# The first two blocks of a convolution and SiLU-MLP kernel: convolution on TensorE, w_out loads in a new order, weight sums one by one

## The chip, the cores and the metric

The kernel runs on one core of a Trainium2 chip. A core has five engines that each take their own instructions in order: TensorE (PE in the profile; its weight loads are PEld), VectorE (DVE), ScalarE (ACT), GpSimd (POOL) and SyncE (SP), which here only issues DMAs. An engine waits at an instruction until the semaphores that it names have been raised by other engines or by DMAs that landed. The metric is the device time of one execution in microseconds (us), lower is better; of several runs the median is taken.

## The reference

Two steps follow each other. `x` is 8 x 4096 x 192 float32. A causal depthwise convolution of 7 taps runs along the 4096 positions; the taps are a softmax over 7 weights for each of 8 heads of 24 channels. Its output is a matrix of 32768 x 192, which goes through an MLP of 2048 hidden units with SiLU:

```python
w = np.exp(w); w = w / (np.sum(w, axis=-1, keepdims=True) + 1e-09)      # 8 heads x 7 taps
out = np.einsum('hk,bskhg->bshg', w, x_unf)                             # 7 shifted copies of x
h = x @ w_in                                                            # 32768x192 @ 192x2048
g = h * (1.0 / (1.0 + np.exp(-h)))
return (g @ w_out).astype(np.float32)                                   # 32768x2048 @ 2048x192
```

The weights arrive as float64 and are used in the kernel after a rounding to float32 that it does itself on the two 32-bit halves.

## The kernel before, in words

**Blocks.** The 32768 rows are worked on in 32 blocks of 1024 rows. Of the 192 channels, the first 128 lie on 128 partitions with 1024 rows on the free axis (`k = 0`: tiles `nat0`, `xt0`, `xs0`). The last 64 are folded into 128 partitions by 512 rows (`k = 1`: `nat1`, `xt1`, `xs1`), partitions 0 to 63 for the first 512 rows and 64 to 127 for the second. A block's input is loaded into `nat`, turned by VectorE into `xt` (`turn_in`), convolved (`conv`: one multiply on ScalarE and six multiply-adds on VectorE, in place in `nat`), and split for the float32r matmuls (`split`) into three parts: `h`, a scaled high part, made by ScalarE; `l`, the rest, made by VectorE; and `d`, a correction, made by VectorE.

**Matmuls of a block.** `w_in` gives 16 tiles of 128 hidden units, counted by `j` (0 to 3) and `c` (0 to 3). For each tile, PE adds `A` (channels 0 to 127, parts h and l), `C` (channels 128 to 191, parts h and l), ScalarE rescales the sum in PSUM (`X`), PE adds the corrections `B` and `E`, and ScalarE applies SiLU into `g` (`S`). From block 1 on, A and B too are done in halves of 64 rows, and after C and after E VectorE copies one column of the PSUM bank into `dot` (`T`, `U`); the next matmul that writes that bank waits for this copy. The output product with `w_out` then needs sums of tiles of `g` (`s` tokens) and sums of tiles of `wd` (the rounded `w_out`, made once by `combine_out`), and matmuls `Q`, which for block b stand in the list of block b + 1.

**Order.** From block 1 on, the order of all work is a list of tokens written by hand (`PLAN`), run once for each block by `step`; a token with a minus sign belongs to the block before, one with a plus to the block after. Each engine takes its instructions in the order in which the Python code emits them (`pin`). Block 0 has its own order, lines 671 to 734, since there the weights are still being rounded.

**Block 0.** Its channels 0 to 127 are convolved on PE with seven diagonal matrices of the taps (`diag`), in two PSUM banks (`banks[0]`, `banks[1]`); `split_pe` reads them there. Its channels 128 to 191 are convolved by `conv` on ScalarE and VectorE. Between these stand the rounding units, `Unit`: units 0 to 7 make `w_b` (even units) and `w_a` (odd units) of j = 0 to 3 from `w_in`, units 8 to 11 make a quarter of `wd` each from `w_out`. `work(u)` does one in three pieces: first `begin(u + 1)` (the exponent of the *next* unit, with two operations on POOL and a sign on ScalarE), mantissa and sticky bit; second `rounded`, three VectorE operations, and where so written the issue of a later load; third `split` into three parts and, for `w_b`, two DMAs (`spread`) that copy parts to the other partitions. The raw words of `w_out` come in four loads, `load_out(0)` to `load_out(3)`, of two DMAs each. They reuse buffers: 0 and 3 lie in the same slots of `g`, 1 where the raw words of `w_in`, j = 2, were (`fin[0:6]`), 2 where those of j = 3 were (`fin[6:12]`).

The up products of block 0 are woven with units (`woven`): during j, the four tiles of j (`tile_steps`) and the pieces of units 2j + 3 and 2j + 4. Tiles 0 to 2 have their A done ahead. After the 16 tiles come the last unit, the input of block 1, and the output product of block 0 by 96 plain float32 matmuls (`down_plain`), three copies and transposes into `fin`, and 12 stores. Then `combine_out(0, 1)` puts all 23 sums and two negations of `wd` on VectorE, and the list of tokens starts with block 1.

Of the kernel before, what the change touches and what calls it, by code (L numbers as in the profile page):

```python
# [18 lines left out]
def kernel(  # L19
# [340 lines left out]

    def combine_out(part, parts):
        work = [*COMBINE_OUT, *((0, s, s, s) for s in NEGATE_OUT)]
        n = (len(work) + parts - 1) // parts
        for sign, to, u, v in work[n * part : n * part + n]:
            to, u, v = (wd[:, :, s, :] for s in (to, u, v))
            if sign:
                vec.tensor_tensor(to, u, v, op=ALU.add if sign > 0 else ALU.subtract)
            else:
                vec.tensor_scalar(to, u, scalar1=-1.0, scalar2=None, op0=ALU.mult)

# [224 lines left out]
    units += [Unit(q, ("o", q), None) for q in range(NJ)]  # L595

    def begin(u):
        if u < len(units):
            units[u].exponent()

    def work(u):

        now = units[u]
        begin(u + 1)
        now.mantissa()
        now.sticky()
        yield
        now.rounded()
        if now.key == ("o", 0):
            load_out(3, sync)  # L610
        yield
        if now.part is not None:
            now.split()
            now.spread()
        yield
# [9 lines left out]

    diag = flat(g_all[:, 0, 7])[:, 0 : K * P].rearrange("p (i c) -> p i c", c=P)

# [4 lines left out]
    def of_work(u):  # L632
        stream = work(u)
        for _ in range(3):
            yield lambda: next(stream, None)
# [35 lines left out]

    for i in range(K):
        act.activation(diag[:, i, :], one_hot, AF.Copy, scale=taps[:, 0, i : i + 1])
    turn_in(0, 0)
    for n in range(2):
        for i in range(K):
            mm(banks[n], diag[:, i, :], xts[0][:, n * TB + i : n * TB + i + TB], i == 0)
    homes.append(homes.pop(0))
    homes.append(homes.pop(0))
    begin(0)  # L680
    first_ = work(0)
    next(first_)
# [86 lines left out]
```

## Time and profile before

| | |
|---|---|
| median of 3 runs | 2268.2 us (2267.3 to 2268.77) |
| the profiled execution | 2267.96 us |
| its span, first to last instruction | 2266.2 us |
| PE busy | 2229.3 us, 98% |
| DVE busy | 1831.4 us, 81% |
| ACT busy | 1302.0 us, 57% |
| POOL busy | 59.5 us, 3% |
| mean granted TensorE clock | 0.991 |

The span is cut off by the first and the last instruction; 1.8 us of the profiled execution's time lie outside it. PE is busy nearly throughout, but its busy time holds slow matmuls too: where the granted clock is 0.50, a matmul takes twice as long. In a row of the timeline stand the start and the length in us, the engine, the line, the operation, out<-in, the count, and in brackets the idle time of the engine just before with what ended it. L142 is the helper through which all operations but the matmuls go, so the rows are told apart by their tiles and shapes.

### The profile page before, as it was taken

Reading aid. Unit: us, or ns where it says so; the run is one execution under the profiler, and the core shown is the slowest. Engines: PE = TensorE matmul, PEld = TensorE weight load, DVE = VectorE, ACT = ScalarE, POOL = GpSimd, SP = SyncE. Lnnn points to the kernel's source line nnn. Section 1 sums busy time; section 2 is a strip of 40 time slices with the busy share of each in tenths; the row PEclk is TensorE's granted clock in tenths of the full one; section 3 lists DMA queues with packets and bytes.
Section 4 is the critical chain, followed back from the end, with each engine's and each line's share of the span. In section 5 each row is a group of like instructions: output and inputs, shape, how many; then the busy total and the mean of one; then the engine's idle time right before and its main releaser. Section 6 shows DMA issues by size and latency. Waiting matters only on the chain.

```text
span 2266.2 us, 47061 instructions
## 1 busy us (share of the span) xinstructions
PE 2229.3 (98%) x19276; PEld 1671.2 (74%) x19276; DVE 1831.4 (81%) x3029; ACT 1302.0 (57%) x2671; POOL 59.5 (3%) x74
## 2 busy tenths in 40 slices
PE   8889999999999999999999999999999999999998
PEld 4357777877777777777777777777777777777775
DVE  8758887788887788887788887888877888877866
ACT  5455556655566655566655566655567655566643
POOL 5400000000000000000000000000000000000000
PEclk9989999999999999999999999999999999999999
DMA  4210111101111101111101111011111011111001
GB/s 110 58 29 15 29 29 29 26 5 29 29 29 29 22 9 29 29 29 29 17 14 29 29 29 29 12 19 29 29 29 29 10 21 29 30 29 29 10 7 29
DMA packets 407273, 61.23 MB, mean 27 GB/s; under 512 B 401937, under 2 KB 405521, under 8 KB 407057
## 3 DMA queue, kind: packets, MB, share of 16 engines
q1 hardware_dynamic: 401840, 57.58, 14.8%
q8 instruction: 150, 2.46, 0.4%
q10 hardware_dynamic: 5216, 0.66, 0.2%
q14 instruction: 67, 0.54, 0.1%
HBM read 31.46 MB, written 25.17 MB: 25 GB/s over the span
## 4 chain that ended last, share of the span: by engine, by line
PE 96%; DVE 2%; DMA 1%; SPq 0%; ACT 0%; issue 0%; DVEq 0%; ACTq 0%
PE ps L451 96%; DVE g L142 1%; SPq L142 0%; DMA fin<-in_moe_w_out_dram 0%; DMA g<-in_moe_w_in_dram 0%; DVE nat L142 0%; DVE fin L142 0%; DVE xs L142 0%; ACT g L142 0%; DVE wd L142 0%; ACT ps L142 0%; DVE w_a L142 0%; DVE w_b L142 0%; ACT xs L142 0%; ACT wd L142 0%
## 5 line engine op out<-in xcount | busy, mean ns | idle before, releaser
L451 PE MATMUL ps<-g,wd 128*64 128x256 f32 (+1 forms) x10112 | 1125.6, 384 | 0.0
L451 PEld LDWEIGHTS ps<-g,wd 128*64 128x64 f32 x10112 | 720.4, 137 | 395.3 <-issue 34.6
L142 DVE TENSOR_TENSOR g<-g 128x1024 f32<-128x1024 f32 x806 | 951.3, 1218 | 9.2 <-PE ps L451 5.7
L451 PE MATMUL ps<-xs,w_a 64*128 64x512 f32 (+1 forms) x6048 | 890.0, 392 | 24.6 <-ACT ps L142 11.4
L142 ACT ACTIVATE ps<-ps 128x512 f32<-128x512 f32 (+1 forms) x1117 | 585.1, 581 | 308.2 <-PE ps L451 262.1
L451 PEld LDWEIGHTS ps<-xs,w_a 64*128 64x128 f32 (+1 forms) x6048 | 633.4, 185 | 126.6 <-ACT ps L142 28.1
L142 ACT ACTIVATE g<-ps 128x512 f32<-128x512 f32 x1024 | 560.9, 615 | 51.0 <-PE ps L451 42.0
L451 PE MATMUL ps<-xs,w_b 64*128 64x512 f32 x3072 | 529.0, 395 | 1.5 <-ACT xs L142 1.3
L142 DVE COPY dot<-ps 128x1 f32<-128x1 f32 x992 | 155.3, 157 | 358.9 <-PE ps L451 349.6
L142 DVE SCALAR_TENSOR_TENSOR nat<-xt,taps,nat 128x512 f32<-128x512 f32 (+1 forms) x378 | 373.2, 1001 | 1.9 <-ACT nat L142 1.4
L451 PEld LDWEIGHTS ps<-xs,w_b 64*128 64x128 f32 x3072 | 324.2, 185 | 53.5 <-issue 17.3
L142 ACT COPY fin<-ps 128x256 f32<-128x256 f32 (+1 forms) x127 | 47.7, 376 | 423.4 <-PE ps L451 423.4
L142 DVE TENSOR_TENSOR fin<-fin,ps 128x256 f32<-128x256 f32 x248 | 95.8, 405 | 19.2 <-PE ps L451 19.2
L142 DVE STREAM_TRANSPOSE fin<-fin 128x256 f32<-128x256 f32 (+1 forms) x189 | 82.9, 440 | 16.4 <-ACT fin L142 15.1
L142 ACT ACTIVATE nat<-xt,taps 128x512 f32<-128x512 f32 (+1 forms) x63 | 58.7, 933 | 16.3 <-DVE xt L142 14.7
L142 DVE STREAM_TRANSPOSE xt<-nat 128x512 f32<-128x512 f32 (+1 forms) x64 | 61.6, 964 | 2.5 <-ACT xt L142 2.5
L142 ACT ACTIVATE xs<-nat 128x512 fp32r<-128x512 f32 (+1 forms) x63 | 53.1, 843 | 17.2 <-DVE nat L142 17.2
L142 DVE SCALAR_TENSOR_TENSOR xs<-xs 128x512 fp32r<-128x512 f32 x65 | 61.0, 938 | 0.3
L142 DVE TENSOR_TENSOR xs<-nat,xs 128x512 fp32r<-128x512 f32 (+1 forms) x63 | 59.7, 948 | 0.7 <-ACT xs L142 0.7
L142 ACT ACTIVATE fin<-ps 128x256 f32<-128x256 f32 x93 | 35.8, 385 | 39.3 <-PE ps L451 39.3
L142 POOL TENSOR_SCALAR g<-g 128x256 int32<-128x256 int32 (+2 forms) x24 | 50.6, 2108 | 33.5 <-DVE g L142 32.5
L142 POOL COPY xt<-xt 128x6 f32<-128x6 f32 x24 | 5.6, 235 | 1507.6 <-DVE dot L142 1426.4
(58 smaller groups left out, 207.7 us busy)
## 6 DMA issues: line engine op xcount, KB each, us to landing
out_dram<-fin SPq DMA_DIRECT2D x244, 96.0 KB, 2.6
nat<-in_x_dram SPq DMA_DIRECT2D x126, 128.0 KB, 2.9
nat<-in_x_dram SPq DMA_DIRECT2D x128, 64.0 KB, 2.3
w_b<-w_b SPq DMA_DIRECT2D x8, 192.0 KB, 3.1
g<-in_moe_w_out_dram SPq DMA_DIRECT2D x4, 384.0 KB, 4.0
fin<-in_moe_w_out_dram SPq DMA_DIRECT2D x4, 384.0 KB, 5.0
g<-in_moe_w_in_dram SPq DMA_DIRECT2D x2, 512.0 KB, 5.2
fin<-in_moe_w_in_dram SPq DMA_DIRECT2D x2, 512.0 KB, 8.5
```

The lines of the kernel that those rows point to most:

```text
L142: return lambda *args, **kw: pin(getattr(self.engine, name)(*args, **kw))
L451: return pin(nc.tensor.matmul(to, lhs, rhs, start=start, stop=True, skip_group_check=True))
```

## The change

There are three parts.

1. **Convolution of block 0 wholly on PE, and a new order at its start.** A second set of seven diagonal matrices (`diag_of(1)`, in slot 6 or 7 of `g`) is made by ScalarE, and channels 128 to 191 are convolved by seven more matmuls into `banks[2]`. `conv(0, 1, ...)`, one operation on ScalarE and six on VectorE, goes away in block 0. The pieces of units 0 to 3 are interleaved with the splits in an order written out by hand; unit 3's first two pieces move ahead of the woven part, where only its last piece is left.
2. **Order of w_out's loads.** Before: 0, 1, 3, 2, where 1 and 2 were issued after the woven parts of j = 1 and j = 2, and 3 in unit 8's second piece. Now each is issued in the second piece of a unit: 1 in unit 5's, 2 in unit 7's, 3 in unit 8's (`LATER`).
3. **Sums of wd spread.** `combine_out` becomes a generator. In block 1's list, one sum is emitted just ahead of each of the block's own `T` and `U` tokens. Twenty-seven such tokens stand in the list without a sign, so all 25 operations go out within block 1; the `drain` at a token `Q` finds no token that begins with Q, since they all carry a sign.

```diff
-    def combine_out(part, parts):
-        work = [*COMBINE_OUT, *((0, s, s, s) for s in NEGATE_OUT)]
-        n = (len(work) + parts - 1) // parts
-        for sign, to, u, v in work[n * part : n * part + n]:
+    def combine_out():
+        for sign, to, u, v in [*COMBINE_OUT, *((0, s, s, s) for s in NEGATE_OUT)]:
...
-                vec.tensor_tensor(to, u, v, op=ALU.add if sign > 0 else ALU.subtract)
+                yield vec.tensor_tensor(to, u, v, op=ALU.add if sign > 0 else ALU.subtract)
...
+    LATER = {2 * NJ - 3: 1, 2 * NJ - 1: 2, 2 * NJ: 3}
...
         now.rounded()
-        if now.key == ("o", 0):
-            load_out(3, sync)
+        if u in LATER:
+            load_out(LATER[u], sync)
...
+    diags = [flat(g_all[:, 0, s_])[:, 0 : K * P].rearrange("p (i c) -> p i c", c=P) for s_ in (6, 7)]
+
+    def diag_of(k):
+        for i in range(K):
+            act.activation(diags[k][:, i, :], one_hot, AF.Copy, scale=taps[:, k, i : i + 1])
+
+    def conv_on_pe(to, k, first):
+        for i in range(K):
+            mm(to, diags[k][:, i, :], xts[k][:, first + i : first + i + TB], i == 0)
+        homes.append(homes.pop(0))
...
     turn_in(0, 1)
     halo_in(0, 2)
-    conv(0, 1, 0)
-    drain(first_)
-    drain(work(1))
-    for what in "hld":
-        split_pe(0, what)
-    for i in range(1, 4):
-        conv(0, 1, i)
-    for what in "hld":
-        split_pe(1, what)
-    for i in range(4, K):
-        conv(0, 1, i)
+    diag_of(1)
+    conv_on_pe(banks[2], 1, 0)
+    next(pieces[0])
+    drain(pieces[0])
+    next(pieces[1])
+    split_pe(0, "h")
+    next(pieces[1])
+    split_pe(0, "l")
+    split_pe(0, "d")
+    drain(pieces[1])
+    next(pieces[2])
+    split_pe(1, "h")
+    next(pieces[2])
+    drain(pieces[2])
+    split_pe(1, "l")
     for i in range(AHEAD):
         up_first("A", i)
-    for what in "hld":
-        split(0, 1, what)
-    drain(work(2))
+    next(pieces[3])
+    split_pe(1, "d")
+    split(0, 1, "h", banks[2])
+    next(pieces[3])
+    split(0, 1, "l", banks[2])
+    split(0, 1, "d", banks[2])
     load_out(0, sync)
     for j in range(NJ):
...
-        if j == 1:
-            load_out(1, sync)
-        if j == 2:
-            load_out(2, sync)
...
-    combine_out(0, 1)
+    combined = combine_out()
     for b in range(1, NB + 3):
         for t in plan:
+            if b == 1 and t[0] in "TU":
+                next(combined, None)
+            if b == 1 and t[0] == "Q":
+                drain(combined)
             step(b, t)
```

**What stands where on VectorE at the start of block 0.** The rows run from unit 1's rounding to the `d` of the channels 128 to 191 (`xs_76`; `xs_75` is that of channels 0 to 127, `nat_72` and `xt_74` are the natural and the turned tile of channels 128 to 191, `g` and `fin` hold the units' words). Before:

```order
L142 TENSOR_SCALAR g<-g 128x512 x5
L142 TENSOR_SCALAR w_a<-g 128x512
L142 TENSOR_TENSOR g<-g,w_a 128x512
L142 TENSOR_SCALAR w_a<-w_a,g 128x512
L142 TENSOR_TENSOR xs_75<-ps,xs_75 128x512
L142 TENSOR_SCALAR xs_75<-xs_75 128x512
L142 TENSOR_SCALAR nat_72<-xt_74,taps,nat_72 128x512 x3
L142 TENSOR_TENSOR xs_75<-ps,xs_75 128x512
L142 TENSOR_SCALAR xs_75<-xs_75 128x512
L142 TENSOR_SCALAR nat_72<-xt_74,taps,nat_72 128x512 x3
L142 TENSOR_TENSOR xs_76<-nat_72,xs_76 128x512
L142 TENSOR_SCALAR xs_76<-xs_76 128x512
```

Now, from unit 3's exponent, which stands after the first bank's l and d and unit 1's split:

```order
L142 TENSOR_SCALAR g<-g 128x512
L142 TENSOR_SCALAR g<-g 128x256 x5
L142 TENSOR_SCALAR w_b<-g 128x256
L142 TENSOR_TENSOR g<-g,w_b 128x256
L142 TENSOR_SCALAR w_b<-w_b,g 128x256
L142 TENSOR_TENSOR xs_75<-ps,xs_75 128x512
L142 TENSOR_SCALAR g<-fin 128x256
L142 TENSOR_SCALAR g<-g 128x512 x2
L142 TENSOR_SCALAR xs_75<-xs_75 128x512
L142 TENSOR_SCALAR g<-g 128x512 x3
L142 TENSOR_TENSOR xs_76<-ps,xs_76 128x512
L142 TENSOR_SCALAR xs_76<-xs_76 128x512
```

The six operations on `nat_72` are gone, and all of unit 2 and two thirds of unit 3 now stand ahead of the `l` (`xs_76<-ps`) for which C waits.

**The queue of SyncE, from the copies of w_b of units 0 and 2 to the loads of block 1.** `fin` holds loads 1 and 2, `g` holds 0 and 3. Before:

```order
L142 DMA w_b<-w_b 64x3x256 x4
L142 DMA g<-in_moe_w_out_dram 128x2x384 x2
L142 DMA w_b<-w_b 64x3x256 x4
L142 DMA fin<-in_moe_w_out_dram 128x2x384 x2
L142 DMA g<-in_moe_w_out_dram 128x2x384 x2
L142 DMA fin<-in_moe_w_out_dram 128x2x384 x2
L142 DMA nat_71<-in_x_dram 32x32x32 x4
```

Now:

```order
L142 DMA w_b<-w_b 64x3x256 x4
L142 DMA g<-in_moe_w_out_dram 128x2x384 x2
L142 DMA w_b<-w_b 64x3x256 x2
L142 DMA fin<-in_moe_w_out_dram 128x2x384 x2
L142 DMA w_b<-w_b 64x3x256 x2
L142 DMA fin<-in_moe_w_out_dram 128x2x384 x2
L142 DMA g<-in_moe_w_out_dram 128x2x384 x2
L142 DMA nat_71<-in_x_dram 32x32x32 x4
```

Load 1 has moved ahead of unit 6's copies, and load 2 ahead of load 3; load 3 is now the one that stands just ahead of block 1's input.

**VectorE from the end of block 0 into block 1.** `fin` holds the output of block 0, `dot` is written by T and U, and the two transposes turn the input of block 2 (tokens `+i.1`, `+i.0`). Before:

```order
L142 STREAM_TRANSPOSE fin<-fin 128x512 x3
L142 TENSOR_TENSOR wd<-wd 128x4x64 x23
L142 TENSOR_SCALAR wd<-wd 128x4x64 x2
L142 COPY dot<-ps 128x1
L142 STREAM_TRANSPOSE xt_74<-nat_72 128x512
L142 STREAM_TRANSPOSE xt_73<-nat_71 128x1024
L142 COPY dot<-ps 128x1 x2
L142 TENSOR_SCALAR nat_72<-xt_74,taps,nat_72 128x512
```

Now:

```order
L142 STREAM_TRANSPOSE fin<-fin 128x512 x3
L142 TENSOR_TENSOR wd<-wd 128x4x64
L142 COPY dot<-ps 128x1
L142 STREAM_TRANSPOSE xt_74<-nat_72 128x512
L142 STREAM_TRANSPOSE xt_73<-nat_71 128x1024
L142 TENSOR_TENSOR wd<-wd 128x4x64
L142 COPY dot<-ps 128x1
L142 TENSOR_TENSOR wd<-wd 128x4x64
L142 COPY dot<-ps 128x1
L142 TENSOR_SCALAR nat_72<-xt_74,taps,nat_72 128x512
```

One sum stands ahead of the first `dot` instead of 25 operations; the two transposes stand where they stood, between the first and the second `dot`.

More of the change, by code (lines that the diff above doesn't have):

```diff
@@ L359, in spread @@
                     )
-    def combine_out(part, parts):
-        work = [*COMBINE_OUT, *((0, s, s, s) for s in NEGATE_OUT)]
-        n = (len(work) + parts - 1) // parts
-        for sign, to, u, v in work[n * part : n * part + n]:
+    def combine_out():
+        for sign, to, u, v in [*COMBINE_OUT, *((0, s, s, s) for s in NEGATE_OUT)]:
             to, u, v = (wd[:, :, s, :] for s in (to, u, v))
             if sign:
-                vec.tensor_tensor(to, u, v, op=ALU.add if sign > 0 else ALU.subtract)
+                yield vec.tensor_tensor(to, u, v, op=ALU.add if sign > 0 else ALU.subtract)
             else:
-                vec.tensor_scalar(to, u, scalar1=-1.0, scalar2=None, op0=ALU.mult)
+                yield vec.tensor_scalar(to, u, scalar1=-1.0, scalar2=None, op0=ALU.mult)
     def heat(times):
@@ L624, in woven @@
                     s_[k]()
-    diag = flat(g_all[:, 0, 7])[:, 0 : K * P].rearrange("p (i c) -> p i c", c=P)
+    diags = [flat(g_all[:, 0, s_])[:, 0 : K * P].rearrange("p (i c) -> p i c", c=P) for s_ in (6, 7)]
[6 more added lines that the diff above has]
+        homes.append(homes.pop(0))
     def drain(stream):
@@ L632, in of_work @@
     def of_work(u):
-        stream = work(u)
-        for _ in range(3):
+        stream = pieces[u] if u < len(pieces) else work(u)
+        for _ in range(1 if u < len(pieces) else 3):
             yield lambda: next(stream, None)
@@ L670, in tile_steps @@
                 yield lambda what=what, k=k: up_first(what, k)
-    for i in range(K):
-        act.activation(diag[:, i, :], one_hot, AF.Copy, scale=taps[:, 0, i : i + 1])
+    diag_of(0)
     turn_in(0, 0)
[L675 to L679, printed above, removed]
+    conv_on_pe(banks[0], 0, 0)
+    conv_on_pe(banks[1], 0, TB)
     begin(0)
-    first_ = work(0)
-    next(first_)
+    pieces = [work(u) for u in range(4)]
+    next(pieces[0])
     turn_in(0, 1)
     halo_in(0, 2)
-    conv(0, 1, 0)
-    drain(first_)
-    drain(work(1))
-    for what in "hld":
-        split_pe(0, what)
-    for i in range(1, 4):
-        conv(0, 1, i)
-    for what in "hld":
-        split_pe(1, what)
-    for i in range(4, K):
-        conv(0, 1, i)
+    diag_of(1)
+    conv_on_pe(banks[2], 1, 0)
+    next(pieces[0])
+    drain(pieces[0])
[10 more added lines that the diff above has]
+    split_pe(1, "l")
     for i in range(AHEAD):
         up_first("A", i)
-    for what in "hld":
-        split(0, 1, what)
-    drain(work(2))
+    next(pieces[3])
[4 more added lines that the diff above has]
+    split(0, 1, "d", banks[2])
     load_out(0, sync)
```

## The prediction

> **What bounds the kernel now.** I read the page first, then the list of what PE waited for, then the granted clock by stretches, and last the timeline of the places that these point to.
>
> ```profile
> span 2266.2 us, 47061 instructions
> ...
> PE 96%; DVE 2%; DMA 1%; SPq 0%; ACT 0%; issue 0%; DVEq 0%; ACTq 0%
> ```
>
> The chain that ends last is PE for 96%. A change in blocks 0 and 1 is worth only what it moves the moment from which PE runs without a pause. PE's waits (total us, times, longest):
>
> ```profile
> PE ps L451 <- ACT ps L142: 11.4, 3, 6.7
> PE ps L451 <- DVE dot L142: 10.0, 2, 9.8
> PE ps L451 <- DVE xs L142: 3.3, 3, 2.8
> PE ps L451 <- ACT xs L142: 1.3, 1, 1.3
> ```
>
> Some 26 us in nine waits. Beside the waits there is the clock; in these rows (a stretch, its length, busy us and instructions by engine, then the granted clock) the column after POOL is PEclk:
>
> ```profile
> 26.20:29.60 3.40, 1.89 (x12) 0.97 (x10) 2.63 (x5) 1.19 (x2) 0.00 (x0) 1.00 0.00 0
> 29.70:39.80 10.10, 5.92 (x18) 3.22 (x14) 9.76 (x20) 4.83 (x10) 6.49 (x4) 0.50 0.41 118
> 39.90:70.50 30.60, 27.41 (x131) 16.50 (x130) 25.30 (x41) 24.15 (x48) 22.75 (x10) 1.00 0.33 94
> 70.60:80.80 10.20, 6.28 (x18) 3.78 (x20) 7.58 (x9) 6.64 (x12) 6.88 (x3) 0.50 0.58 105
> 80.90:128.60 47.70, 45.52 (x214) 15.51 (x210) 30.15 (x36) 9.75 (x17) 7.13 (x4) 1.00 0.04 7
> 128.70:142.20 13.50, 5.90 (x28) 4.21 (x30) 9.86 (x26) 3.58 (x7) 0.00 (x0) 0.50 0.57 94
> 142.30:172.00 29.70, 29.70 (x264) 26.14 (x262) 18.64 (x44) 28.76 (x59) 0.19 (x1) 1.00 0.01 1
> ```
>
> Three pauses are each followed by a half clock, to 39.9, 80.9 and 142.3. From 142.3 on PE is busy 29.70 of 29.70 us. So the change acts on the time until then, in two stretches: the up products of block 0, whose end is the first matmul of the output product, and the passage into block 1.
>
> **Part 1: the start of block 0.** The rows of before, VectorE first:
>
> ```profile
> 14.81 3.14 DVE L142 SCALAR_TENSOR_TENSOR g<-g 128x512 int32<-128x512 int32 x4
> 19.18 0.69 DVE L142 SCALAR_TENSOR_TENSOR w_a<-w_a,g 128x512 fp32r<-128x512 f32 x1
> 20.32 0.69 DVE L142 TENSOR_TENSOR xs<-ps,xs 128x512 fp32r<-128x512 f32 x1 [0.46 <-ACT xs L142]
> 21.66 2.32 DVE L142 SCALAR_TENSOR_TENSOR nat<-xt,taps,nat 128x512 f32<-128x512 f32 x3
> 29.57 0.62 DVE L142 TENSOR_SCALAR g<-g 128x512 int32<-128x512 int32 x2
> 33.33 0.42 DVE L142 SCALAR_TENSOR_TENSOR w_b<-w_b,g 128x256 fp32r<-128x256 f32 x1
> 34.41 3.13 DVE L142 SCALAR_TENSOR_TENSOR g<-g 128x512 int32<-128x512 int32 x4
> ```
>
> ```profile
> 7.65 12.93 PE L451 MATMUL ps<-xt,g 128*128 128x512 f32 x28
> 28.98 1.12 PE L451 MATMUL ps<-xs,w_b 64*128 64x512 f32 x6 [0.22 <-DVE xs L142]
> 33.33 0.42 ACT L142 ACTIVATE w_b<-g 128x256 fp32r<-128x256 f32 x1 [4.57 <-DVE g L142]
> 33.66 1.06 ACT L142 ACTIVATE ps<-ps 128x512 f32<-128x512 f32 x2
> 34.29 1.28 PE L451 MATMUL ps<-xs,w_a 128*128 128x512 f32 x2 [4.18 <-ACT ps L142]
> ```
>
> Tile 0's rescale X (33.66) stood behind unit 2's w_b on ScalarE, which waited for VectorE to reach unit 2. B of tile 0 (34.29) is where the steady stream of tiles begins. Now unit 2 stands earlier, and X waits only for C, which waits for the l of channels 128 to 191.
>
> On PE: the 14 convolution matmuls show as 28 records of 0.43 us, so the seven new ones add 6.0 us and end at 26.6; A of tiles 0 to 2 (12 matmuls of 0.23) ends at 29.4. On VectorE the order is the same until 17.95 (end of the first row). Then come l and d of bank 0 (2 x 0.69), unit 1's split (17.99 to 19.87: 1.88), unit 2 (29.57 to 33.75: 4.18), l of bank 1 (0.69), unit 4's exponent and unit 3's mantissa (33.75 to 34.41: 0.66), unit 3's four operations (3.13), d of bank 1 (0.69), and the l in question (0.69): 17.95 + 13.3 = 31.25. PE is there first, by 1.6 us, so the new matmuls are hidden behind VectorE; without that cover they would cost up to 6.0 us. The multiply-adds taken off VectorE are 2 x 2.32 = 4.64 us; 0.7 us of that is not felt, since VectorE stood still for ScalarE between them. ScalarE pays seven diagonal copies while it has nothing else; its h of bank 0 and of bank 1 come free at 14 and 20.6, before VectorE asks.
>
> So C's second half goes at 31.3, X after half a microsecond (28.98: three pairs in 1.12 with their drain), and B 0.63 after X began (34.29 less 33.66): 32.5 in place of 34.29.
>
> **Part 2: the loads.**
>
> ```profile
> 57.70 0.93 DVE L142 TENSOR_SCALAR w_a<-g 128x512 fp32r<-128x512 f32 x1
> 65.74 0.98 SPq L142 DMA_DIRECT2D fin<-in_moe_w_out_dram  x2
> 66.76 8.48 SPq L142 DMA_DIRECT2D nat<-in_x_dram  x8
> 73.12 1.03 DVE L142 TENSOR_SCALAR g<-fin 128x768 int32<-128x768 int32 x2 [6.87 <-DMA fin<-in_moe_w_out_dram]
> 74.53 1.27 PE L451 MATMUL ps<-xs,w_a 128*128 128x512 f32 x2 [6.72 <-ACT ps L142]
> 77.53 1.46 DVE L142 SCALAR_TENSOR_TENSOR wd<-g 128x768 f32<-128x768 f32 x1
> 83.97 16.53 PE L451 MATMUL ps<-g,wd 128*64 128x512 f32 x76
> ```
>
> Load 2 was issued at 65.74 and VectorE, already waiting, went on at 73.12. PE's 6.72 us are the same wait, since X stands behind unit 10's sign on ScalarE. Now load 2 is issued when unit 7 is rounded, where VectorE begins the split at 57.70, and is asked for where VectorE stood at 66.25: 8.5 us for a load that took 7.4 with its queue full. It is hidden. Load 1 too goes out earlier and is asked for at the same place.
>
> Late next is load 3: it now goes out after unit 8, just ahead of block 1's loads, as load 2 did, and I give it the same 7.4 us. VectorE's work until it asks is one unit, 73.12 to 78.99, 5.9 us, plus start-up: a wait of 1.2 us. If the packets are shared otherwise, 0 to 3.
>
> From 34.29 to 83.97 are 49.68 us. They hold 6.72 and 0.5 of waiting (the third wait on ACT: 11.4 less 6.7 and 4.18), and half clock from 34.29 to 39.85 (5.56) and from 74.53 to 80.85 (6.32), which cost half of that, 5.94. The stream itself is 36.5 us. Now: 32.5 + 36.5 + 1.2 = 70.2. To this comes the clock. PE pauses about 1.6 us ahead of C and half a microsecond ahead of B; in before it fell after a stretch in which PE was busy 1.89 of 3.40 us. I let it fall once and last as long as then: 2.8. The output product starts at 73.0 in place of 83.97: a gain of 11.0. Ends: 69 (no fall, no wait) and 77 (a longer wait, and a second fall after it), a gain of 7 to 15.
>
> VectorE is not the bound there: split of unit 3 comes at 32 in place of 37.54 (end of the row of 34.41), so it leads PE by more than before. After the units it has until the end of the output product for block 1's convolution, in a stretch where it was busy 30.15 of 47.70 us (80.90 to 128.60).
>
> **Part 3: the sums.**
>
> ```profile
> 126.70 9.07 DVE L142 TENSOR_TENSOR wd<-wd 128x256 f32<-128x256 f32 x23
> 135.70 0.62 SPq L142 DMA_DIRECT2D nat<-in_x_dram  x1
> 138.75 1.84 DVE L142 STREAM_TRANSPOSE xt<-nat 128x512 f32<-128x512 f32 x2 [2.51 <-ACT xt L142]
> 140.51 0.38 DVE L142 COPY dot<-ps 128x1 f32<-128x1 f32 x2
> 140.76 2.54 PE L451 MATMUL ps<-xs,w_a 64*128 64x512 f32 x14
> 143.11 0.16 DVE L142 COPY dot<-ps 128x1 f32<-128x1 f32 x1 [1.55 <-PE ps L451]
> ```
>
> The last line of the view of the tile `nat`, over the eight loads of block 2's input:
>
> ```profile
> DMA to landing us min/median/max: 2.4/2.6/3.2
> ```
>
> The 25 operations seem to cost PE its 9.8 us. But behind the first dot stand the two transposes of block 2's input, and its last load was issued at 135.70 as the last of eight behind block 0's 12 stores; with 2.6 us to land it is there at 138.3. The transpose began at 138.75, put down to ScalarE's halo copy, yet the load came just before it. Stores and loads hang on the end of block 0's output product, which the sums don't touch. So VectorE, freed of the sums, stands at that transpose until 138.4 to 138.75 all the same, and PE, after the matmuls up to the second dot (they took from 136.3 to 140.8), stands too. I count no gain: instead the second dot comes after one sum, 0.42 us later (9.07 over 23, with overlap); I take 0.4.
>
> The clock turns this into a loss. Before, PE worked at half clock from 136.3 behind that cover, and only 140.76 to 142.25, 1.5 us, fell on the path. Now it pauses some 11 us just ahead of the second dot, and the 6.0 us of half clock (136.3 to 142.25) begin after it: (6.0 - 1.5) / 2 = 2.2 more.
>
> The other 23 operations, 9.7 us, go into 142 to 172, where VectorE has 29.70 - 18.64 = 11.1 us free and stands ahead of its dots waiting for PE (1.55 in the row of 143.11). Nearest that row they cost nothing, at worst all 9.7; I take 0.6, for the dots that come behind a multiply-add and a sum.
>
> Sum: -11.0 + 0.4 + 2.2 + 0.6 = -7.8 us on the profiled execution's 2267.96, which stands 0.24 under the median: 2260.4 from the median. The rest of the 32 blocks has the same instructions.
>
> A rule against my clock terms: the Trainium skill, TensorE: Matmul & The Clock Gate, Part 1, says that the clock goes by free-running windows of about 3.4 us, falls after an idle window and rises after one busy window. By that the pause ahead of C would not lower it, and the half clock into block 1 would cost (3.4 - 1.5) / 2 = 1.0: in all 4.0 us less, 2256.4. The trace disagrees in part: it fell at 29.65 without an idle stretch of 3.4 us, and rose only 5.6 to 6.3 us after work began.
>
> **The rivals.**
> - *The clock does not fall at the start.* For it: PE's pauses are 2 us in all where before there were 2.83, 1.29 and 4.18. Against: 1.89 busy of 3.40 was enough to fall. It gives 2.8 less: 2257.6.
> - *The transposes don't hold the second dot* (the halo copy did, and the loads come sooner). For it: the row names ACT. Against: the landing at 138.3. PE would then go on at once, 9 us earlier: about 2251.
> - *The load's wait only moves* to load 3, since block 1's loads share the queues: a wait like the old 6.7 in place of 1.2, with its half clock. It takes 5.5 to 8 of the 11: 2266 to 2268, no change that can be told.
> - *Slower: dots too late in block 1.* Where a sum and a multiply-add of 1.27 us stand ahead of a dot, PE pauses up to 1.7 us. Were PE busy as little as in the row of 26.20 (1.89 of 3.40), the clock would stay at 0.50 until 172: the work of 147 to 172 at half speed costs 25 us more, 2285. It decides from 16 us of half clock on. Against: the 11.1 us free.
>
> **How the numbers follow.** Chances: the forecast 0.50 (its own range 2257 to 2264), the clock that holds 0.18, the free dots 0.06, the moved wait 0.16, slower 0.07, the rest 0.03 on either side. About 0.2%, 4.5 us, is what a measurement of this kernel can tell from no change, so faster means under 2263.7: the first three and part of the rest, 0.75; within, 0.17; slower, 0.08. The range leaves out the free dots and the slower case: 2253 to 2267.
>
> **What would show it.** The first `ps<-g,wd` matmul near 73 us; no wait of PE of 6 us ahead of it; in the list of waits, DVE dot still near 10 us, and ahead of the transposes of block 2's input an idle VectorE, ended by a DMA; half clock for 5 us or so after it; and no wait on dot after that. I am wrong if PE leaves block 0's end without that pause, or if VectorE reaches the l of channels 128 to 191 well after 32 us.

## The result and the profile after

| | before | after |
|---|---|---|
| median | 2268.2 us (2267.3 to 2268.77) | 2257.48 us (2257.36 to 2257.99) |
| the profiled execution | 2267.96 us | 2257.62 us |
| its span | 2266.2 us | 2255.7 us |
| mean granted TensorE clock | 0.991 | 0.995 |

The ratio is 0.9953, with a 95% interval of 0.9939 to 0.9968: 10.7 us faster, where 7.8 were forecast. The time lies in the range and 2.9 us under the predicted one. It is nearest the rival in which the clock does not fall at the start (2257.6), but that agreement hides terms missed on both sides, as the steps show.

What PE waits for in the changed kernel (total us, times, longest); the line of its matmuls is now L449:

```profile
PE ps L449 <- DVE dot L142: 12.7, 3, 11.7
PE ps L449 <- ACT ps L142: 1.1, 3, 0.4
PE ps L449 <- DVE xs L142: 0.3, 1, 0.3
```

The 11.4 us behind ScalarE's rescale are down to 1.1; the wait for the dots has grown from 10.0 to 12.7. By stretches (length, busy us by engine in the order PE, PEld, DVE, ACT, POOL, then the granted clock):

```profile
29.72:33.13 3.41, 2.96 (x17) 1.41 (x15) 3.31 (x8) 2.52 (x6) 0.18 (x1) 1.00 0.18 66
33.14:68.20 35.06, 34.62 (x164) 20.91 (x164) 34.16 (x49) 34.96 (x70) 30.26 (x13) 1.00 0.45 113
109.62:126.47 16.85, 3.98 (x30) 2.34 (x30) 3.88 (x9) 3.16 (x7) 0.00 (x0) 0.76 0.57 94
128.71:132.12 3.41, 3.41 (x18) 2.66 (x16) 1.64 (x5) 1.73 (x5) 0.00 (x0) 0.50 0.00 0
132.20:172.00 39.80, 39.68 (x346) 29.71 (x344) 33.99 (x72) 32.02 (x64) 0.19 (x1) 1.00 0.13 22
```

The clock is full until the passage into block 1 and falls once, from 118.47 to 132.12; of the three half-clock stretches of before, two are gone. The start and the loads in the timeline:

```profile
7.65 18.99 PE L449 MATMUL ps<-xt,g 128*128 128x512 f32 x42
29.33 0.68 DVE L142 TENSOR_TENSOR xs<-ps,xs 128x512 fp32r<-128x512 f32 x1
30.07 0.98 PE L449 MATMUL ps<-xs,w_b 64*128 64x512 f32 x6 [0.25 <-DVE xs L142]
31.24 0.98 PE L449 MATMUL ps<-xs,w_a 128*128 128x512 f32 x2 [0.20 <-ACT ps L142]
57.69 0.88 SPq L142 DMA_DIRECT2D g<-in_moe_w_out_dram  x2
65.68 0.56 DVE L142 TENSOR_SCALAR g<-g 128x768 int32<-128x768 int32 x1
66.86 0.98 PE L449 MATMUL ps<-xs,w_a 128*128 128x512 f32 x2 [0.44 <-ACT ps L142]
68.20 2.37 PE L449 MATMUL ps<-g,wd 128*64 128x512 f32 x10
```

The steady stream of tiles begins at 31.24 (before 34.29), load 3 is asked for at 65.68 without any wait, and the output product starts at 68.20 (before 83.97). Then the passage:

```profile
109.55 0.73 PE L449 MATMUL ps<-xs,w_b 64*128 64x512 f32 x4
110.92 0.38 DVE L142 TENSOR_TENSOR wd<-wd 128x256 f32<-128x256 f32 x1
116.88 5.15 SPq L142 DMA_DIRECT2D nat<-in_x_dram  x8
124.20 1.84 DVE L142 STREAM_TRANSPOSE xt<-nat 128x512 f32<-128x512 f32 x2 [12.82 <-DMA nat<-in_x_dram]
126.26 0.15 DVE L142 COPY dot<-ps 128x1 f32<-128x1 f32 x1
126.47 2.08 PE L449 MATMUL ps<-xs,w_a 64*128 64x512 f32 x8 [11.74 <-DVE dot L142]
```

VectorE, with only one sum ahead of the first dot, stands 12.82 us for block 2's input, and PE 11.74 behind the second dot.

Laid over each other matmul by matmul, the changed kernel is ahead of the one before by 15.77 us at the first matmul of the output product, 14.29 behind the second dot, 12.34 at 132.6 where its clock is back, 11.6 from 150 on, and 10.5 at the end. So the first two parts of the change bring 15.8 us, and the passage gives 4.2 of them back; the last 1.1 us go little by little over the 2100 us that follow. Executions of one kernel differ by more than that (2265.85 to 2269.13 for the kernel before beside the first four experiments), so this last part need not come from the change.

### The profile page after: what moved, and what is told of

The parts are those of the page before. It is cut to its first block, busy times and chain, and to the rows that moved or that the text cites. A ratio compares the mean times of both kernels' runs of the same rounds, so it can differ in the third digit from the quotient of the medians.

```text
span 2255.7 us, 47089 instructions
## 1 busy us (share of the span) xinstructions
PE 2230.7 (99%) x19290; PEld 1665.5 (74%) x19290; DVE 1825.9 (81%) x3023; ACT 1304.1 (58%) x2677; POOL 59.7 (3%) x74
## 4 chain that ended last, share of the span: by engine, by line
PE 97%; DVE 1%; ACT 1%; SPq 1%; DMA 0%; issue 0%; DVEq 0%
PE ps L449 97%; SPq L142 1%; DVE g L142 1%; DMA nat<-in_x_dram 0%; ACT g L142 0%; ACT ps L142 0%; DVE xs L142 0%; ACT wd L142 0%; DVE fin L142 0%; DVE xt L142 0%; DVE wd L142 0%; DVE w_a L142 0%; DVE w_b L142 0%; DVE nat L142 0%; DVE dot L142 0%
## 5 line engine op out<-in xcount | busy, mean ns | idle before, releaser
L449 PE MATMUL ps<-g,wd 128*64 128x256 f32 (+1 forms) x10112 | 1125.6, 384 | 0.0
L449 PEld LDWEIGHTS ps<-g,wd 128*64 128x64 f32 x10112 | 720.4, 137 | 395.1 <-issue 34.7
L449 PE MATMUL ps<-xs,w_a 64*128 64x512 f32 (+1 forms) x6048 | 890.6, 391 | 13.9 <-DVE dot L142 12.7
L449 PEld LDWEIGHTS ps<-xs,w_a 64*128 64x128 f32 (+1 forms) x6048 | 632.5, 185 | 118.1 <-DVE dot L142 27.2
L449 PE MATMUL ps<-xs,w_b 64*128 64x512 f32 x3072 | 530.8, 393 | 0.3 <-DVE xs L142 0.3
L142 DVE SCALAR_TENSOR_TENSOR nat<-xt,taps,nat 128x1024 f32<-128x1024 f32 (+1 forms) x372 | 368.4, 1004 | 2.1 <-ACT nat L142 1.4
L449 PEld LDWEIGHTS ps<-xs,w_b 64*128 64x128 f32 x3072 | 325.7, 184 | 53.9 <-issue 17.4
L142 ACT ACTIVATE nat<-xt,taps 128x1024 f32<-128x1024 f32 (+1 forms) x62 | 57.9, 936 | 16.2 <-DVE xt L142 14.7
L142 DVE TENSOR_TENSOR xs<-nat,xs 128x1024 fp32r<-128x1024 f32 (+1 forms) x62 | 58.9, 950 | 0.0
L142 ACT ACTIVATE xs<-nat 128x1024 fp32r<-128x1024 f32 (+1 forms) x62 | 52.5, 846 | 10.9 <-DVE nat L142 10.9
L142 ACT COPY xt<-xt 64x6 f32<-64x6 f32 x56 | 10.9, 195 | 69.6 <-DVE xt L142 69.0
```

What stands on the lines that cost most here:

```text
L142: return lambda *args, **kw: pin(getattr(self.engine, name)(*args, **kw))
L449: return pin(nc.tensor.matmul(to, lhs, rhs, start=start, stop=True, skip_group_check=True))
```

## The experiments

Theory: the waits at the start and for load 2 were on the path and are gone; the spread sums are a loss, since the second dot waits for block 2's loads, which stand behind block 0's stores. Eight kernels were timed, on three chips. The kernel before, run beside them on the same chip, took 2267.29 us (beside the experiments on the sums at once, the old load order, the old start and block 2's input), 2267.45 (beside the next three to be run) and 2266.98 (beside the last). Where two of the kernels are compared, each is first set against the kernel before beside it; by that measure the changed kernel is 10.7 us faster.

### All sums at once again

```diff
     combined = combine_out()
+    drain(combined)
     for b in range(1, NB + 3):
```

> The changed kernel with part 3 undone: all 25 sums of wd stand ahead of the first dot again. Theory (the loads of block 2 hold the second dot, the sums lay behind them): the second dot comes at the same place after the output product, one sum (0.4 us) earlier; the matmuls ahead of it run at half clock behind the wait, and the half clock is over some 5 us earlier in the work, 2.0 us; the 0.7 us that PE lost behind dots later in block 1 goes. 3.1 us faster than the changed kernel: 2254.4. Rival (the 9.8 us that PE waited for the first dot were the sums' own): 9 us slower, 2266.5.

Measured: 2252.29 us (2251.53 to 2252.87), ratio 0.9934 [0.9919, 0.9948]. This is 15.0 us faster than the kernel before, and the changed kernel 10.7: the spread sums cost it 4.3 us. The theory's direction holds; its 3.1 us were 1.2 short. The timeline of the kernel with all sums at once, VectorE and then PE:

```profile
110.90 9.07 DVE L142 TENSOR_TENSOR wd<-wd 128x256 f32<-128x256 f32 x23
122.86 1.84 DVE L142 STREAM_TRANSPOSE xt<-nat 128x512 f32<-128x512 f32 x2 [2.42 <-ACT xt L142]
```

```profile
120.49 2.07 PE L449 MATMUL ps<-xs,w_a 64*128 64x512 f32 x8 [9.77 <-DVE dot L142]
124.95 2.38 PE L449 MATMUL ps<-xs,w_a 64*128 64x512 f32 x14
```

PE waits 9.77 us at the first dot, yet reaches the matmul behind the second dot at 124.95, 1.5 us before the changed kernel does. Behind it 2.1 us more come from the half clock, which here lies mostly under the wait (it ends at 126.23), and 0.7 from dots without a sum ahead of them: 4.3 in all. The term that was short is the second dot, for which 0.4 had been expected; the last experiment shows where its other 1.1 us come from.

### The loads of w_out in the old order

```diff
-    LATER = {2 * NJ - 3: 1, 2 * NJ - 1: 2, 2 * NJ: 3}
+    LATER = {2 * NJ: 3}
...
+        if j == 1:
+            load_out(1, sync)
+        if j == 2:
+            load_out(2, sync)
```

> The changed kernel with w_out's loads in the order of before (load 1 after j = 1, load 2 after j = 2, load 3 in unit 8). Theory (the loads are worth the wait and its half clock): PE waits some 6.5 us for load 2 ahead of the last tiles, and half clock costs 3 more: the output product starts at 77.5 to 78 in place of 68.2, 2267. Rival (the start alone moved things, load 2 would land in time now): no wait over 2 us, 2257.5 to 2260.

Measured: 2266.37 us (2264.43 to 2268.14), ratio 0.9996 [0.9986, 1.0005]: without the new order of the loads nearly all of the gain is gone. Its timeline, SyncE, VectorE and PE apart:

```profile
61.02 0.98 SPq L142 DMA_DIRECT2D fin<-in_moe_w_out_dram  x2
62.04 9.77 SPq L142 DMA_DIRECT2D nat<-in_x_dram  x8
```

```profile
69.57 1.03 DVE L142 TENSOR_SCALAR g<-fin 128x768 int32<-128x768 int32 x2 [8.04 <-DMA fin<-in_moe_w_out_dram]
```

```profile
70.98 1.27 PE L449 MATMUL ps<-xs,w_a 128*128 128x512 f32 x2 [7.85 <-ACT ps L142]
```

VectorE asks for load 2 4.7 us earlier than in the kernel before, but the load lands only 3.6 us earlier, at 69.4 and 8.4 us after its issue. So VectorE waits 8.04 us in place of the 6.87 of before, and PE 7.85. The output product starts at 80.26, 12.06 us after that of the changed kernel. That is 7.41 of wait (7.85 less the 0.44 that is there now), half of the 5.94 us between 70.98 and the clock's rise at 76.92, and half of the 3.41 us of half clock that this kernel shows at the start (32.55 to 35.96): 12.09. Of the 12.06 us, 1.0 come back in the passage and 1.3 little by little behind it. Which of the three loads that moved brings the gain was not run apart; the wait in the rows is for load 2.

### The start of before with the new loads and sums

```diff
-    diag_of(1)
-    conv_on_pe(banks[2], 1, 0)
...
+    conv(0, 1, 0)
+    drain(first_)
+    drain(work(1))
+    for what in "hld":
+        split_pe(0, what)
+    for i in range(1, 4):
+        conv(0, 1, i)
...
```

> The changed kernel with the start of before (channels 128 to 191 of block 0 convolved on ScalarE and VectorE, units in the old order), new loads and spread sums kept. Theory (the start is worth the 3.05 us by which the first B came earlier and the half clock behind it): B at 34.3, half clock after it, output product at 74, 2263.3. Rival (the start is bound elsewhere, by the loads alone): output product at 68 to 70, 2258 to 2260.

Measured: 2261.08 us (2260.55 to 2262.01), ratio 0.9973 [0.9963, 0.9984]. Against the same kernel before, the changed one is 10.7 us ahead and this one 6.2: the new start is worth 4.5 us. The time lies between the theory's 2263.3 and the rival's 2258 to 2260. The output product starts 6.72 us later than in the changed kernel, 1.7 more go in it, and the passage gives 1.5 back (the stall of the last experiment is not there) and 1.2 behind it, where the half clock is shorter; 1.3 more come back little by little over the other blocks. Where its stream begins, in PE's timeline:

```profile
33.87 1.27 PE L449 MATMUL ps<-xs,w_a 128*128 128x512 f32 x2 [4.34 <-ACT ps L142]
```

First B is 2.63 us later. The clock falls behind the stretch from 30.62 to 34.03, in which PE is busy 0.16 of 3.41 us, and one window of half clock, to 37.44, costs 1.7 more; a second one, from 74.99 to 78.40, is the 1.7 within the output product.

### The new order, with channels 128 to 191 on ScalarE and VectorE

```diff
-    diag_of(1)
-    conv_on_pe(banks[2], 1, 0)
+    conv(0, 1, 0)
...
     split_pe(0, "d")
+    for i in range(1, 4):
+        conv(0, 1, i)
...
     split_pe(1, "l")
+    for i in range(4, K):
+        conv(0, 1, i)
```

> The changed kernel with its new order of units, loads and sums, but with channels 128 to 191 of block 0 convolved by one operation on ScalarE and six multiply-adds on VectorE, which stand between the splits as they did before. Theory: the six operations of 0.77 us stand ahead of the l for which C waits; first B at 35.9 in place of 31.24, and PE, which has nothing to do for about 6 us ahead of C, gets half clock behind it: 4.6 us, or 7.4 with the clock: 2262 to 2265. Rival: the order alone made the start shorter, and VectorE hides the six operations in its own waits: 2257.5 to 2259.

Measured: 2261.37 us (2260.07 to 2263.41), ratio 0.9973 [0.9961, 0.9984], within 0.3 us of the old start and 0.6 below the theory's range; the rival's 2257.5 to 2259 lie further off. So of the new start it is the convolution on PE that brings the gain, and the new order of units without it nothing that shows. Whether the convolution on PE would bring it in the old order too was not run. By stretches, with the columns as above:

```profile
18.07:21.49 3.42, 1.31 (x4) 0.37 (x2) 3.31 (x6) 0.00 (x0) 0.00 (x0) 1.00 0.81 168
31.73:35.14 3.41, 1.25 (x8) 0.48 (x6) 3.34 (x6) 0.39 (x1) 0.64 (x1) 1.00 0.18 69
38.55:41.97 3.42, 3.42 (x10) 2.27 (x11) 3.28 (x8) 1.62 (x4) 3.10 (x3) 0.50 0.03 5
```

Behind each of the first two rows the clock falls; the third is the last one at half clock. First B comes at 35.39, 4.15 us later than in the changed kernel (forecast 4.6), and 6.6 us of half clock follow. The output product is 6.74 us later. The seven matmuls on PE might do two things: free VectorE of six multiply-adds, and keep PE busy so that the clock stays up. The second fall is VectorE's: in the window ahead of it PE stands 2.16 us for the late `l` of channels 128 to 191. The first comes where PE has no convolution to do, and the last experiment shows what such a fall costs.

### Only the sums spread, in the kernel before

```diff
-    combine_out(0, 1)
+    combined = combine_out()
...
+            if b == 1 and t[0] in "TU":
+                next(combined, None)
```

> The kernel before, with the sums of wd spread one by one over block 1 and nothing else changed. Theory: the second dot is held by block 2's loads as in the changed kernel, the half clock falls behind the wait in place of under it, the dots of block 1 come later: a loss of 3 to 4.4 us on 2267.3, 2270.5 to 2272. Rival: the sums were on the path, and spreading them gives their 9 us back: about 2259.

Measured: 2269.76 us (2268.71 to 2271.55), ratio 1.001 [1.0, 1.0019]: 2.3 us slower than the kernel before, which is at the edge of what the interval can tell from no change, under the 3 to 4.4 expected, and far from the rival's gain. Its timeline at the passage, VectorE and then PE:

```profile
137.84 1.84 DVE L142 STREAM_TRANSPOSE xt<-nat 128x512 f32<-128x512 f32 x2 [11.43 <-DMA nat<-in_x_dram]
```

```profile
124.59 0.73 PE L449 MATMUL ps<-xs,w_b 64*128 64x512 f32 x4
140.11 3.35 PE L449 MATMUL ps<-xs,w_a 64*128 64x512 f32 x14 [10.35 <-DVE dot L142]
```

The 25 operations left the passage, 9 us of VectorE's time, and PE is at the matmul behind the second dot 15.52 us after block 0's output product, where before it was 15.43. By alignment with the kernel before, the second dot costs 0.1 us, the half clock behind it 1.2 and the dots of block 1 0.8: 2.1 in all.

### Block 2's input loaded ahead of block 0's stores

```diff
+    for i in range(8):
+        step(2, f"ld.{i}")
     accs = [homes[k] for k in range(NK)]
```

> The changed kernel with the eight loads of block 2's input issued ahead of block 0's output product, so that they don't stand behind its 12 stores. Theory (these loads hold the transposes ahead of the second dot): PE's wait of 11.7 us falls to about 1, the clock stays up (2.8 us of half clock saved): 13.9 us faster, 2243.6. Rival (ScalarE's halo copy or the sums hold that dot): less than 2 us, 2255.5 to 2257.5.

Measured: 2243.56 us (2242.07 to 2245.58), ratio 0.9896 [0.9881, 0.9911], as the theory had it. This kernel beats both: 23.7 us against the one before, 13.0 more than the changed kernel. SyncE, VectorE and PE, and PE's waits:

```profile
93.16 4.89 SPq L142 DMA_DIRECT2D nat<-in_x_dram  x8
109.24 7.50 SPq L142 DMA_DIRECT2D out_dram<-fin  x12
```

```profile
112.94 1.84 DVE L142 STREAM_TRANSPOSE xt<-nat 128x512 f32<-128x512 f32 x2 [1.66 <-ACT xt L142]
```

```profile
115.21 1.89 PE L449 MATMUL ps<-xs,w_a 64*128 64x512 f32 x14 [0.57 <-DVE dot L142]
```

```profile
PE ps L449 <- DVE dot L142: 1.5, 3, 0.7
```

The eight loads go out while the queue of SyncE is empty, the transpose begins at 112.94 in place of 124.20, and the 11.74 us are 0.57. The clock does not fall at all. So in the changed kernel it was these loads that held the second dot.

### Both: early loads and all sums at once

```diff
+    for i in range(8):
+        step(2, f"ld.{i}")
     accs = [homes[k] for k in range(NK)]
...
     combined = combine_out()
+    drain(combined)
```

> Loads of block 2's input ahead of block 0's stores, as in e4_x_ahead_of_stores, and all 25 operations on wd in one go ahead of block 1, as in e1_sums_at_once. Theory: each of the two things alone is enough to hold PE for some 10 us at a dot, so the loads go early for nothing: PE waits 9.8 us for the first dot again, the clock falls behind it, and the time is that of e1_sums_at_once, 2252 to 2253. The spreading of the sums is then a loss alone and a gain only with the early loads (2243.6). Rival: the two are independent, the loss of 5 us by spread sums and the gain of 14 us by early loads add up: 2238.4.

Measured: 2252.89 us (2252.63 to 2253.84), ratio 0.9935 [0.992, 0.9949], as the theory had it. PE's timeline at the first dot:

```profile
120.69 2.08 PE L449 MATMUL ps<-xs,w_a 64*128 64x512 f32 x8 [9.77 <-DVE dot L142]
```

VectorE, at the transpose behind that dot:

```profile
122.78 1.84 DVE L142 STREAM_TRANSPOSE xt<-nat 128x512 f32<-128x512 f32 x2 [2.14 <-ACT xt L142]
```

The loads have long landed here (by 100.0), yet the transpose comes as late as with the late loads (122.86). It waits for ScalarE's halo copy, which stands on ScalarE behind a rescale of the first dot's matmuls. With the three kernels above, this makes a table of four, in us gained against the kernel before run beside each:

| | 25 operations at once | spread |
|---|---|---|
| block 2's loads behind the stores | 15.0 | 10.7 |
| block 2's loads ahead of them | 14.6 | 23.7 |

Either thing alone holds PE for some 10 us. To spread the sums is a loss of 4.3 us with the late loads and a gain of 9 with the early ones; to load early brings nothing with the sums at once and 13 us without (13.9 where the two kernels are laid over each other matmul by matmul, up to 140).

### The stores that stall

One term was left over: the passage takes 16.92 us in the changed kernel (109.55 to 126.47), against 15.52 with the sums alone spread. The first fence is the landing time of block 0's 12 stores in the changed kernel (the view of the tile `out_dram`); the second, from its view of DMA queues between 113.6 and 117.8, one packet of 16 KB on q8 in that stretch (packets, MB, share of 16 engines):

```profile
DMA to landing us min/median/max: 1.7/1.9/4.0
```

```profile
q8 instruction: 1, 0.02, 1.5%
```

In the first nine profiles (both kernels and the seven above) this packet runs either 5.0 to 5.8 us after the first matmul behind block 0's output product (the changed kernel, the old load order, the early loads) or 14.6 us and more after it (the other six). In the first three the slowest store takes 3.6 to 4.0 us, in the six 1.9. q8 moves 150 packets for PE's 38,597 matmuls and weight loads, 257 each, so it may be PE's own instructions. Counted in the traces, this packet runs when PE has begun 938 to 940 matmuls and weight loads in the five profiles with the whole convolution on PE, and 926 in the four others, at whatever time that is. If so, the changed kernel's 29 more of them, for the convolution, set the place.

```diff
     def conv_on_pe(to, k, first):
-        for i in range(K):
+        taps_used = range(K) if k == 0 else range(1)
+        for i in taps_used:
```

> The changed kernel with six of the seven matmuls left out that convolve channels 128 to 191 of block 0 (only one tap is applied there): PE has 24 instructions fewer (each of these matmuls is two records, each with a weight load) ahead of the passage into block 1; all else stands as in the changed kernel. The question is why block 0's stores stall there for 2 us, behind which block 2's loads and with them the second dot come late. Theory: the 16 KB packet of the queue q8 is PE's own instructions (150 packets for 38,597 PE instructions and weight loads, 257 each), and in the changed kernel PE, with 29 more of them, asks for it just ahead of the second dot, in the middle of the stores, and not behind it. With 24 fewer it is asked for behind the second dot again: the packet runs some 16 us after the end of block 0's output product, no store takes over 2 us to land, and from the end of the output product to the matmul behind the second dot are 15.4 us in place of 16.85. Rival: the packet and the stall come from the new order of the sums or of the loads, whatever PE's count: the packet at 5 to 6 us, a store of 3.6 us or more, 16.85 us. The time is 2255.5 to 2256.5 by the theory and 2257.5 by the rival, and up to 3 more by either if the clock falls at the start, where PE has 2.6 us less to do.

Measured: 2255.15 us (2254.46 to 2257.91), ratio 0.9953 [0.9936, 0.997]. That is 11.8 us faster than the kernel before, 1.1 more than the changed kernel, too little for the time alone to decide; the trace does. The packet now runs 16.6 us after that matmul, when PE has begun 930. Over the same 12 stores the landing time, and then PE's timeline at both ends of the passage:

```profile
DMA to landing us min/median/max: 1.7/1.9/1.9
```

```profile
109.29 0.73 PE L449 MATMUL ps<-xs,w_b 64*128 64x512 f32 x4
124.82 3.36 PE L449 MATMUL ps<-xs,w_a 64*128 64x512 f32 x14 [10.36 <-DVE dot L142]
```

15.53 us from one to the other: the stall is gone with 24 PE instructions, though sums and loads stand as in the changed kernel. The packet's place goes by PE's count, and where it falls among the stores, 1.4 us of the passage go with it. How a 16 KB packet holds the stores for 2 us is not shown.

This kernel also tells the two uses of the convolution on PE apart, since VectorE is freed in it, while PE has one matmul in place of seven. The clock fell ahead of C, at 24.70, and was back at 28.12, before the stream began:

```profile
30.99 0.99 PE L449 MATMUL ps<-xs,w_a 128*128 128x512 f32 x2 [0.20 <-ACT ps L142]
```

First B comes 0.25 us earlier than in the changed kernel. So what pays at the start is that VectorE is freed; that PE is kept busy by the new matmuls brought nothing that shows.

## Why the prediction was right or wrong

| step | forecast | measured |
|---|---|---|
| first B, where the stream begins | 32.5 | 31.24 |
| the stream and its waits, without load 3 | 36.5 | 36.96 |
| wait for load 3 | 1.2 | 0 |
| a fall of the clock at the start | 2.8 | 0 |
| output product starts | 73.0 | 68.20 |
| second dot, against before | +0.4 | +1.5 |
| half clock behind it | +2.2 | +1.95 |
| dots of block 1 behind sums | +0.6 | +0.75 |
| the other blocks | 0 | +1.1 |
| sum against before | -7.8 | -10.5 |

The start. That VectorE's `l` of channels 128 to 191 sets the moment of C, that the new matmuls are covered (they end at 26.64, forecast 26.6, and without six of them B came only 0.25 us earlier) and that X and B follow at once, held. The `l` began at 29.33 where 30.56 was worked out. Of these 1.2 us, 0.5 come from a load of `w_in` at 8.74 in place of 9.69, with which VectorE is through unit 1's exponent and mantissa at 17.45 and not 17.95; the rest from adding durations of instructions that overlap their neighbours by some 0.08 us each: from 17.45 to 29.33 are 11.88 us, where the sum had 12.61.

The clock. Here the choice was wrong. The forecast let it fall because it had PE pause 1.6 us ahead of C and half a microsecond ahead of B. VectorE came 1.2 us earlier, so the pauses were 0.25 and 0.20, and the emptiest window at the start (29.72 to 33.13) had PE busy for 2.96 of 3.41 us. The rival named the outcome and its reason, that PE's pauses are small. It was closer than it looks. Five profiles have this start (the changed kernel, both with sums at once, the old load order, the early loads): PE waited for the `l` 0.25 us in the first, not at all in the next two, and 1.45 and 1.16 us in the last two; first B came between 30.94 and 31.43; and with the old load order the clock did fall, behind this window:

```profile
29.14:32.55 3.41, 2.21 (x10) 1.16 (x12) 3.31 (x7) 1.89 (x4) 0.00 (x0) 1.00 0.35 130
```

There it stayed down for one window, half of which, 1.7 us, is the price; the 2.8 of the forecast took the length from before, where PE had paused for 4.18 us more. In the three experiments that convolve channels 128 to 191 on ScalarE and VectorE it fell twice each at the start; in the kernel before, which has the same start as two of them, it fell once.

The loads. Load 2 was hidden, as forecast. Load 3 was given the 7.4 us that load 2 took before; its two DMAs landed by 63.9, 6.2 us after the issue, while VectorE needed 8.0 us from 57.69 to the question at 65.68, not 5.9. The term of 1.2 is 0, which the range of 0 to 3 held. The 7.4 us were not load 3's to expect: before, load 2 did not only stand ahead of block 1's input but also right behind load 3, as SyncE's row there shows (load 2 follows at 65.74).

```profile
64.81 0.88 SPq L142 DMA_DIRECT2D g<-in_moe_w_out_dram  x2
```

In the three kernels with that order load 2 landed 7.3 to 8.4 us after its issue; in the seven in which load 3 goes out alone ahead of block 1's input, it landed after 4.2 to 6.2. The stream's 36.5 us came out as forecast: the measured 36.96 hold the 0.44 us of the third wait on ScalarE's rescale, which the sum had taken out and which stayed. The rival in which the wait moves to load 3 did not happen.

The sums. That they would gain nothing, because the second dot waits for block 2's loads, is shown three times: by the row of the transpose, by early loads that bring 13 us, and by the sums spread alone, 2.3 us slower. The row of before had named ScalarE's halo copy, and the prediction set the landing a moment earlier against it. In fact both held the transpose at once. The last load landed at 138.31, and on ScalarE before, the copy ended at 138.36, behind a rescale that had waited for PE:

```profile
137.55 0.58 ACT L142 ACTIVATE ps<-ps 128x512 f32<-128x512 f32 x1 [11.52 <-PE ps L451]
138.16 0.20 ACT L142 COPY xt<-xt 64x6 f32<-64x6 f32 x1
```

With the first dot free, the copy is done early (at 113.00 in the changed kernel) and the loads alone are left; with the loads early and the sums at once, the copy alone is left, at 122.75. So the forecast for the spread sums held, but by this early loads alone would not have helped the kernel before, which was not run. The rival of free dots was wrong as long as the loads stay late. Of the 1.5 us at the second dot, 1.4 are the stores' stall, which no step had; without it the term is 0.1. The half clock cost 1.95 us, near the 2.2 forecast, and 1.2 where it ended 4.1 us after PE began.

The slower rival, dots too late in block 1, did not occur: PE is busy 39.68 of 39.80 us from 132.20 to 172. It rested on a clock that would stay down, and with pauses as small as these it did not.

So the sign held, and so did the working of each part but for the clock at the start and the price of load 3. The three terms that were too dark (-1.3 at the start, -2.8 for the clock, -1.2 for load 3) are 5.3 us; the second dot with its stall (1.1 more than forecast), the wait of 0.44 and the slow loss of 1.1 us over the other 31 blocks give back some 2.6 of it. That the sum came within 2.9 us is in part luck, since these cancel. What the slow loss is stays open: 0.05% of the time, in instructions that are the same in both kernels.

**The rule that was weighed.** The prediction set the Trainium skill's page TensorE: Matmul & The Clock Gate, Part 1 (free-running windows of 3.41 us, a fall after an idle window, a rise after a busy one) against the rise 5.6 to 6.3 us after work began and said that the trace disagrees in part. With ten profiles it agrees on the rise, but for one window. All half-clock stretches that ended within a kernel lasted 3.41, 6.83, 10.24 or 13.65 us, one to four windows, and each of the 22 rises came at the end of a window in which PE was busy for 87% or more; one window of 94% did not lift the clock (the new order without the convolution on PE, 35.14 to 38.55). The rise came 3.0 to 6.6 us after work resumed, by where the edge lies: 3.0 with the old load order (138.82 to 141.78), 5.65 here (126.47 to 132.12), 6.6 in that new order (35.39 to 41.97). At half clock the work did not take quite twice as long, as was reckoned throughout: what took 5.7 us in the changed kernel from 126.47 on took 3.1 with the early loads, at full clock. On the fall the runs go further than the page: it came also behind windows that were far from idle, with PE busy for 56% ahead of the C of before (the stretch 26.20 to 29.60 of the prediction) and for 70% in the kernel with the old start, just ahead of its output product,

```profile
71.58:74.99 3.41, 2.39 (x10) 0.93 (x11) 3.38 (x4) 3.41 (x7) 3.33 (x2) 1.00 0.48 76
```

and it never came behind one above 70%. Under that it did not always come: before shows a window of 46% that kept the clock,

```profile
22.80:26.21 3.41, 1.58 (x7) 1.32 (x8) 3.31 (x6) 0.00 (x0) 0.00 (x0) 1.00 0.00 0
```

so busy time as the profile records it is not the whole measure.

## What to carry to other kernels

Where an engine's wait is named in the profile, ask what stands behind it on the same engine before taking it away: here 25 operations covered a late load, and spreading them lost 4.3 us until the load was moved too, when the same edit gained 9. Loads for the block after next were better issued ahead of a block's stores, while the queue was empty. A pause of PE can cost twice: behind a window of 3.41 us with 30% of it empty or more, up to 6.6 us of work at half clock followed here. But half clock costs only where the work that it slows is on the path; at the start of the last experiment it cost nothing.

## What was not expected of the hardware

A fetch of instructions can fall among a kernel's own transfers. One packet of 16 KB on q8, which comes about every 257 PE instructions, ran in the middle of 12 stores of 64 KB; four of the stores then took 3.4 to 4.0 us to land in place of 1.9, and PE reached the matmul behind the second dot 1.4 us later. Twenty-four PE instructions more or less ahead of it, in another part of the program, decided on it here. And a load's time to land is not its own: two DMAs of 384 KB took 7.3 us right behind two others before, and 6.2 us without these after, with block 1's input behind them both times.
